# The sums of the token weights leave for DRAM in six pieces, spread over a later stretch of the program, in place of one piece

## The chip, the cores and the metric

The kernel runs on one core of a Trainium2 chip. The core has a matrix engine (TensorE, PE in the profile), a vector engine (VectorE, DVE), an activation engine (ScalarE, ACT), a general engine (GpSimd, POOL) and a synchronisation engine (SyncE, SP) that mostly issues transfers. DMA transfers are issued by SP, ACT and POOL, each on a queue of its own. The metric is the device time of one launch in microseconds (us), lower is better, as the median of several runs. All arithmetic here is float32.

## The reference, cut to what matters

Two blocks stand one behind the other. The first filters a sequence of 3008 positions in the frequency domain, for each of 8 batches and 256 channels; the second is an MLP mixer on the result, first over positions ("tokens"), then over channels.

```python
X = np.fft.rfft(x, axis=1)                       # x: (8, 3008, 256)
y = np.fft.irfft(X * (filt_r + 1j * filt_i), n=3008, axis=1)
xt = y.transpose(0, 2, 1)
h = np.maximum(xt @ w_tok1, 0.0) @ w_tok2        # (3008, 256), (256, 3008)
u = y + h.transpose(0, 2, 1)
h2 = np.maximum(u @ w_ch1, 0.0) @ w_ch2          # (256, 1536), (1536, 256)
return (u + h2).astype(np.float32)
```

The weights arrive as 64-bit floats and are turned into float32 on the chip.

## The kernel before, in words

**The filter.** The transforms are done as matrix products in two stages. The batches form five groups (`GROUPS`, L56: batch 0; 1 and 2; 3 and 4; 5 and 6; 7), and `dft` (L557) runs one group. It is a generator: each `yield` ends a small step. First come the "a" units: rows of `x` are loaded by SP into the three buffers `filts` (L489), multiplied by a table on TensorE (L530), copied by ScalarE and written to a DRAM scratch `z_tmp` (L537 to L541). Then the same three buffers are cleared by GpSimd (L694) and used for the filter's values. For each of 16 pairs `c` SP issues eight loads of filter rows (`filt_pair`, L221 to L228), one load of a table and the loads of `z_tmp` into a tile `t` (`t2_load`, L621 to L632: eight for the first pair, four for each later one). `b_pair` (L668) multiplies the table by `t` on TensorE (L523) and by the filter on VectorE (L674); `join` and `bi_pair` follow, and the result goes to another scratch, `g_tmp` (L689).

**The mixer.** `mix` (L1046) is the main loop. It runs over 288 items, which the code counts with `i`: 8 batches, in each 6 column blocks `m` of up to 512 positions, in each 6 pairs `jp` of channel tiles ("channel pairs"). An item is a fixed series of TensorE products (L936, L970, L952), with the VectorE additions of a fast 2x2 product scheme (L914) and ScalarE's relu (L957) between them. Each item has three places at which the loop at the bottom of the program puts in one step of the next group's `dft`. So the filter for batches 1 and 2 runs between the products of batch 0. The order is written out by hand (`tc.manual_schedule()`), each engine executes its own instructions in that order, and the waits between engines follow from the tiles.

**Token weights.** Batch 0 uses the first token weight directly, as `w1` in SBUF. From batch 1 on the same 2x2 scheme is used, which needs, for each of 12 pairs of slices (`AP`), seven matrices: three that are slices of `w1` as they are and four sums. They are made once while batch 0 runs and kept in a DRAM scratch, `w1_d` (`w1_tmp`). `w1_sums` (L755) returns the list of steps: the raw slices are written to DRAM (L761, L762), sixteen GpSimd operations make the sums in place (L765), and `sums_out` (L773) writes all of them with one DMA from the GpSimd queue (L774). The loop takes one step at item 4 and up to six at each of items 5, 6 and 7 (L1080 to L1083), so that the sums and the DMA are done with item 7. In the program's order that is just behind the last "a" units of group (1, 2), ahead of the clearing of `filts` (L694) on GpSimd. The seven matrices of a pair are read back by `w1_load` (L778) on the SP queue into the same SBUF space, from item 25 on (L1123).

**The second token weight** is treated alike, but already one step per item: `to_dram` (L1074) holds 24 closures of `w2_sums` (L878), four for each `m`: the raw parts to DRAM (L887, L888), two additions (L884), two more (L895, L884), the sums to DRAM (L900). One is taken at the end of each item from item 8 on (L1142).

**Results.** `finish` (L973) adds up a column block and writes it to the output by 16 DMAs on the GpSimd queue (L1017).

Of the kernel before, what the change touches and what calls it, by code (L numbers as in the profile page):

```python
# [42 lines left out]
JP = JT // 2  # L43
# [8 lines left out]
AP = A // 2  # L52
# [75 lines left out]
def kernel(  # L128
# [11 lines left out]
    nc = tc.nc  # L140
# [296 lines left out]
    def convert_middle():  # L437
        advance(middle)
        sum_up()

    def convert_end(copy_now=True):
        ended[0] += 1
        advance(end)
        if copy_now:
            copies()
        fill(5)
# [295 lines left out]
    def t4_load(b, c, lo=PARTS[0], hi=P, queue=nc.sync):  # L742
        if lo == 0:
            t4[b, c] = t4p.tile([P, TC4, D], FP32, tag="t4", name="t4")
        queue.dma_start(t4[b, c][lo:hi], rows_of(g_d, b)[lo:hi, ts(c, TC4), :])
# [9 lines left out]
    def w1_sums():  # L755

        w = w1.rearrange("p (j r) (t n) -> p j r t n", r=2, n=P)
        to = w1_d.rearrange("j p s n -> p j s n")

        def raw_out():  # L760
            nc.gpsimd.dma_start(to[:, :, 0], w[:, :, 0, 0])  # L761
            nc.gpsimd.dma_start(to[:, :, 1:3], w[:, :, 1])  # L762

        def pool(out, in0, in1, op):
            return lambda: nc.gpsimd.tensor_tensor(out=out, in0=in0, in1=in1, op=op)  # L765

        todo = [raw_out]
        for j in range(0, AP, 3):
            c11, c21, c12, c22 = (w[:, j:j + 3, r, t] for r in range(2) for t in range(2))
            todo += [pool(c22, c21, c22, ALU.add), pool(c21, c11, c21, ALU.subtract),  # L770
                     pool(c11, c22, c11, ALU.subtract), pool(c12, c12, c11, ALU.subtract)]

        def sums_out():  # L773
            nc.gpsimd.dma_start(to[:, :, 3:7], w.rearrange("p j r t n -> p j (r t) n"))  # L774

        return todo + [sums_out]

    def w1_load(j):  # L778
        nc.sync.dma_start(w1_ring[:, j % W1S], w1_d[j])
# [94 lines left out]
    def w2m_load(m):  # L874
        hw = width(m) // 2
        nc.sync.dma_start(w2m[m % 2][:, :, 0:hw], w2_d[m, :, :, 0:hw])

    def w2_sums(m):  # L878

        w = width(m)  # L880
        hw = w // 2
        r = w2[:, :, ds(m * 512, w)]
        b11, b12, b21, b22 = (r[:, t, ds(j * hw, hw)] for t in range(2) for j in range(2))
        sub = lambda out, in0, in1: nc.gpsimd.tensor_tensor(out=out, in0=in0, in1=in1, op=ALU.subtract)  # L884

        def raw_out():
            nc.gpsimd.dma_start(w2_d[m, :, 0, 0:hw], b11)  # L887
            nc.gpsimd.dma_start(w2_d[m, :, 1:3, 0:hw], r[:, 1, :].rearrange("p (s n) -> p s n", s=2))  # L888

        def t13():  # L890
            sub(b22, b22, b12)
            sub(b12, b12, b11)

        def t24():
            nc.gpsimd.tensor_tensor(out=b11, in0=b22, in1=b11, op=ALU.add)  # L895
            sub(b21, b11, b21)

        def sums_out():
            for t in range(2):
                nc.gpsimd.dma_start(w2_d[m, :, ds(3 + 2 * t, 2), 0:hw], r[:, t, :].rearrange("p (s n) -> p s n", s=2))  # L900

        return [raw_out, t13, t24, sums_out]
# [122 lines left out]
    def u_part(b, m, i):  # L1025
        if i == 0:
            uts[b, m] = up.tile([P, DH, 512], FP32, tag="u", name="u")
        (u_quarter if b else u_unit)(b, m, h1s[b], uts[b, m], i)

    def v_steps(b, m):  # L1030
        vts[b, m] = vp.tile([P, 4, 256], FP32, tag="v", name="v")
        t13, t2, t4_ = u_sums(uts[b, m], vts[b, m], width(m))

        def t24():
            t2()
            t4_()

        return [t13, t24]
# [7 lines left out]
    def mix(next_ready):  # L1046

        wait = []
        pos, hhs, tts = {}, {}, {}

        def loads(b):
            if b + 1 < B and next_ready(b):
                for c in wait:
                    t4_load(b + 1, c)
                wait.clear()


        own = ({(4, 2): (0, 1)}, {(3, 0): (0,), (4, 0): (1,), (4, 2): (2, 3)})
        new = {(JP - 2, 0): (0, 1), (JP - 1, 0): (2, 3)}

        def u_parts(b, m, jp, place):
            parts = own[b > 0] if m + 1 < MT else new if b + 1 < B else {}
            now = parts.get((jp, place), ())
            b, m = (b, m + 1) if m + 1 < MT else (b + 1, 0)
            for part in now:
                u_part(b, m, part)
            if now and now[-1] == max(p for ps in parts.values() for p in ps):
                if m:
                    wait.append(m)
                todo_v.extend(v_steps(b, m))  # L1070
                if b and (b, m) < (B - 1, MT - 2):
                    w2m_load((m + 2) % MT)

        to_dram = [f for m in range(MT) for f in w2_sums(m)]  # L1074
        w1_todo = w1_sums()
        items = [(b, m, jp) for b in range(B) for m in range(MT) for jp in range(JP)]
        n = MT * JP
        for i in range(len(items) + 1):
            now, old = i < len(items), i >= 1
            if JP - 2 <= i < JP + 2:  # L1080
                for _ in range(6 if i > JP - 2 else 1):
                    if w1_todo:
                        w1_todo.pop(0)()  # L1083
            if i and ended[0] < len(tiles):
                convert_middle()
                convert_end(False)
                convert_middle()
            if now:
                b, m, jp = items[i]
                if i % n == 0:  # L1090
                    wait.append(0)
                w = width(m)
                hhs[i] = hp.tile([P, 4, 256], FP32, tag="hh", name="hh")
                g = [bank("pg").rearrange("p (s n) -> p s n", s=2) for _ in range(2)]
                s = up_first(jp, uts[b, m], vts[b, m], w, g)
                up_middle(hhs[i], w, g, s)
            while todo_h1:
                todo_h1.pop()()
            one_step()
            if old:  # L1100
                bo, mo, jo = items[i - 1]
                tts[i - 1] = tp.tile([P, 4, 256], FP32, tag="t", name="t")
                for f in h_sums(hhs[i - 1], tts[i - 1], width(mo)):
                    f()
                down(mo, jo, 0, hhs[i - 1], tts[i - 1], pos.setdefault((bo, mo), []))
            if now:
                u_parts(b, m, jp, 0)
            copies()
            yield b, i % n, 0
            if ended[0] < len(tiles):  # L1110
                if i == 0:
                    convert_middle()
                convert_end(False)
            if now:
                up_last(jp, uts[b, m], vts[b, m], w, g, s, hhs[i])
                if b + 1 < B and i % n == n - 4:
                    t4_sums(b + 1, 0)
            one_step()
            if now and i % n == n - 1:
                one_step()  # L1120
            if now and b + 1 < B:
                if n - 4 - W1S <= i % n < n - 4:
                    w1_load(i % n - (n - 4 - W1S))  # L1123
                if i % n == n - 4:
                    t4_sums(b + 1, 1)
            copies()
            loads(b)
            yield b, i % n, 1
            if old:
                down(mo, jo, 1, hhs.pop(i - 1), tts.pop(i - 1), pos[bo, mo])  # L1130
                if jo == JP - 1:
                    todo_v.extend(finish(bo, mo, uts[bo, mo], pos[bo, mo]))
                    one_step()
                    one_step()
            if now:
                if b + 1 < B and i % n == n - 4:
                    h1s[b + 1] = token_product(b + 1)
                u_parts(b, m, jp, 2)
                if jp == JP - 1:
                    while todo_v and m + 1 == MT:  # L1140
                        one_step()
                if i >= 8 and to_dram:  # L1142
                    to_dram.pop(0)()
                if i in (28, 29):
                    w2m_load(i - 28)
            loads(b)
            yield b, i % n, 2
        while todo_v:
            one_step()

    with tc.manual_schedule():
# [61 lines left out]
        group, todo, done = -1, iter(()), True  # L1213

        def next_ready(b):
            return done or b != GROUPS[group][-1]
# [4 lines left out]
        n = MT * JP  # L1221
        for b, i, place in mix(next_ready):
            if group + 1 < len(GROUPS) and b == GROUPS[group + 1][0]:
# [4 lines left out]
                todo = iter(()) if done else dft(GROUPS[group + 1]) if group else second  # L1228
# [46 lines left out]
```

## Time and profile before

| What | Value |
|---|---|
| Median of 3 runs | 2457.22 us (2456.94 to 2457.75) |
| The profiled execution's own time | 2455.61 us |
| Its span, first to last instruction | 2453.8 us |
| Mean granted TensorE clock | 0.993 |
| TensorE busy | 2402.2 us, 98% of the span |
| VectorE busy | 1937.0 us, 79% |
| ScalarE, GpSimd busy | 687.3 us, 28%; 620.9 us, 25% |
| The write of the sums (L774) | 3072 KB, issued at 217.1 us, 1084 ns on GpSimd, 13.3 us to landing |

Times inside the profile count from the start of the span. The profile shows, for each engine, what ended its idle time; for TensorE nearly all of the span is work, so that any place where it stood still is of interest. "Granted clock" is the share of the full clock at which TensorE ran. A matmul's end is modelled, since matmuls are pipelined.

### The profile page before, as it was taken

Reading aid. Unit: us, or ns where it says so; the run is one execution under the profiler, and the core shown is the slowest. Engines: PE = TensorE matmul, PEld = TensorE weight load, DVE = VectorE, ACT = ScalarE, POOL = GpSimd, SP = SyncE. Lnnn points to the kernel's source line nnn. Section 1 sums busy time; section 2 is a strip of 40 time slices with the busy share of each in tenths; the row PEclk is TensorE's granted clock in tenths of the full one; section 3 lists DMA queues with packets and bytes.
Section 4 is the critical chain, followed back from the end, with each engine's and each line's share of the span. In section 5 each row is a group of like instructions: output and inputs, shape, how many; then the busy total and the mean of one; then the engine's idle time right before and its main releaser. Section 6 shows DMA issues by size and latency. Waiting matters only on the chain.

```text
span 2453.8 us, 35566 instructions
## 1 busy us (share of the span) xinstructions
PE 2402.2 (98%) x12340; PEld 1973.3 (80%) x12340; DVE 1937.0 (79%) x3684; ACT 687.3 (28%) x1355; POOL 620.9 (25%) x1110
## 2 busy tenths in 40 slices
PE   7998999999999999999999999999999999999998
PEld 4665676977878787987888878897888888898887
DVE  7796878787887888778888888777788788777776
ACT  5742222133222222123221222213222222212222
POOL 7486233113111211211121112112212112112121
PEclk8999999999999999999999999999999999999999
DMA  9986446453443322535344223433325121411100
GB/s 215 247 232 201 123 126 179 147 161 116 121 138 90 86 82 73 167 109 168 94 121 129 86 69 84 155 93 118 98 82 150 50 71 46 148 63 30 39 15 20
DMA packets 187339, 278.65 MB, mean 114 GB/s; under 512 B 35405, under 2 KB 125211, under 8 KB 187160
## 3 DMA queue, kind: packets, MB, share of 16 engines
q1 hardware_dynamic: 140952, 212.56, 29.2%
q0 software_dynamic: 34608, 53.83, 8.2%
q10 hardware_dynamic: 11600, 10.00, 1.3%
q8 instruction: 98, 1.61, 0.3%
q14 instruction: 81, 0.66, 0.1%
HBM read 193.52 MB, written 82.72 MB: 113 GB/s over the span
## 4 chain that ended last, share of the span: by engine, by line
PE 87%; DVE 6%; DMA 3%; issue 1%; ACT 1%; POOL 1%; SPq 0%; ACTq 0%; DVEq 0%; POOLq 0%
PE ps_po L970 33%; PE ps_pg L936 18%; PE ps_pg L952 14%; PE ps_b L523 5%; PE ps_b L802 3%; PE ps_acc L857 3%; PE ps_acc L802 2%; PE ps_b L857 2%; PE ps_b L835 2%; PE ps_acc L835 2%; DVE t L914 1%; PE ps_acc L523 1%; DVE hh L914 1%; PE ps_b L751 1%; DVE u L914 1%
## 5 line engine op out<-in xcount | busy, mean ns | idle before, releaser
L1017 POOL DMA_DIRECT2D out_dram<-r x752 | 409.5, 553 | 1647.4 <-ACT hh L957 1135.5
L914 DVE TENSOR_TENSOR hh<-ps_pg,s 128x512 f32<-128x512 f32 (+3 forms) x864 | 481.6, 585 | 233.3 <-ACT s L939 230.7
L957 ACT ACTIVATE hh<-hh 128x512 f32<-128x512 f32 (+1 forms) x576 | 347.7, 621 | 949.6 <-DVE hh L914 949.6
L970 PE MATMUL ps_po<-t,wc 128*128 128x256 f32 (+1 forms) x2304 | 548.1, 381 | 4.7 <-DVE t L914 3.8
L970 PEld LDWEIGHTS ps_po<-t,wc 128*128 128x128 f32 x2304 | 427.5, 190 | 131.5 <-DVE t L914 44.2
L970 PE MATMUL ps_po<-hh,wc 128*128 128x256 f32 (+1 forms) x1728 | 414.0, 375 | 1.4 <-POOL wc L382 0.8
L936 PE MATMUL ps_pg<-v,wc 128*128 128x256 f32 (+1 forms) x1728 | 413.5, 375 | 0.1
L970 PEld LDWEIGHTS ps_po<-hh,wc 128*128 128x128 f32 x1728 | 326.5, 190 | 42.9 <-ACT s L939 3.6
L936 PEld LDWEIGHTS ps_pg<-v,wc 128*128 128x128 f32 x1728 | 326.8, 190 | 40.9 <-DVE v L914 3.0
L952 PE MATMUL ps_pg<-u,wc 128*128 128x256 f32 (+1 forms) x1152 | 295.2, 379 | 0.7 <-DVE hh L914 0.7
L914 DVE TENSOR_TENSOR t<-t,hh 128x256 f32<-128x256 f32 (+1 forms) x576 | 246.6, 428 | 19.8
L952 PEld LDWEIGHTS ps_pg<-u,wc 128*128 128x128 f32 x1152 | 214.9, 190 | 57.6 <-DVE hh L914 25.1
L914 DVE TENSOR_TENSOR s<-ps_pg,hh 128x512 f32<-128x512 f32 (+1 forms) x288 | 196.0, 681 | 30.7 <-DVE hh L914 0.9
L939 ACT COPY s<-ps_pg 128x256 f32<-128x256 f32 (+1 forms) x288 | 106.0, 368 | 346.2 <-PE ps_pg L936 343.3
L914 DVE TENSOR_TENSOR t<-hh 128x512 f32<-128x512 f32 (+1 forms) x288 | 193.4, 672 | 0.6 <-ACT hh L957 0.6
L936 PE MATMUL ps_pg<-u,wc 128*128 128x256 f32 (+1 forms) x576 | 171.8, 380 | 3.9 <-DVE hh L914 3.9
L952 PE MATMUL ps_pg<-v,wc 128*128 128x256 f32 (+1 forms) x576 | 168.8, 375 | 0.0
L936 PEld LDWEIGHTS ps_pg<-u,wc 128*128 128x128 f32 x576 | 106.3, 190 | 35.6 <-DVE hh L914 20.5
L914 DVE TENSOR_TENSOR u<-ps_acc,u 128x256 f32<-128x256 f32 (+1 forms) x84 | 46.2, 550 | 93.9 <-PE ps_acc L857 86.5
L952 PEld LDWEIGHTS ps_pg<-v,wc 128*128 128x128 f32 x576 | 109.2, 190 | 12.5
L914 DVE TENSOR_TENSOR u<-ps_b,u 128x512 f32<-128x512 f32 (+2 forms) x126 | 74.4, 591 | 28.9 <-PE ps_b L857 26.7
L857 PE MATMUL ps_acc<-w 128*128 128x256 f32 (+1 forms) x336 | 85.2, 376 | 0.0
(149 smaller groups left out, 2716.4 us busy)
## 6 DMA issues: line engine op xcount, KB each, us to landing
w<-w_tmp SPq DMA_DIRECT2D x84, 448.0 KB
w<-w_tmp SPq DMA_DIRECT2D x35, 896.0 KB
out_dram<-r POOLq DMA_DIRECT2D x696, 32.0 KB, 3.2
t<-g_tmp SPq DMA_DIRECT2D x42, 512.0 KB
g_tmp<-t SPq DMA_DIRECT2D x96, 192.0 KB
t<-z_tmp SPq DMA_DIRECT2D x180, 96.0 KB
z_tmp<-t SPq DMA_DIRECT2D x60, 256.0 KB
filt<-in_x_dram SPq DMA_DIRECT2D x90, 128.0 KB
```

Source lines behind the costliest of these rows:

```text
L523: nc.tensor.matmul(outs(i, j), stat(i, j), mov(i, j), start=True, stop=True)
L751: nc.tensor.matmul(acc[:, t, :], w1[:, a, ts(t, P)], t4[b, a // TC4][:, a % TC4, :], start=(a == 0 and t == 0), stop=(a == A - 1 and t == ...
L802: nc.tensor.matmul(ps[:, at], w[:, n], mov, start=(j == 0 and i in (0, 2)), stop=(j == AP - 1 and i >= 5))
L835: nc.tensor.matmul(ps[:, ds(q * P, n)], t4[b, c][:, r, ts(dh, P)], wai[:, 0:n], start=(first and q == 0), stop=(not first and q == 3))
L857: nc.tensor.matmul(ps[:, ds(j * hw, hw)], h1[:, n, :], w2m[m % 2][:, at, 0:hw], start=(i < 2 and j == 0), stop=(j == len(todo) - 1))
L914: nc.vector.tensor_tensor(out=out, in0=in0, in1=in1, op=op)
L936: nc.tensor.matmul(ps[:, 0:hw], chan[0][:, jp, n, :], mov, start=True, stop=True)
L939: nc.scalar.copy(out=s[:, 0], in_=g[0][:, 0, 0:hw])
L952: nc.tensor.matmul(ps[:, 0:hw], chan[0][:, jp, n, :], mov, start=True, stop=True)
L957: nc.scalar.activation(out=hs, in_=hs, func=AF.Relu)
L970: nc.tensor.matmul(po[i][:, j, 0:hw], chan[1][:, jp, n, :], mov, start=(jp == 0 and first == 1), stop=(jp == JP - 1 and last == 1))
L1017: q.dma_start(bass.AP(tensor=ob.tensor, offset=ob.offset + row * D + g * cw, ap=[[N1 * D, 32], [D if h else -D, n], [1, cw]]), blocks[ts(g ...
```

## The change

The one DMA of the sums is cut into six, each for two of the twelve pairs. `w1_sums` returns two lists, the raw write with the sixteen operations, and the six DMAs. The loop takes the first list as before (items 4 to 7), and then one DMA at the start of items 13, 15, 17, 19, 21 and 23. The sixteen operations, the place of `w1_load` and all else stay.

```diff
-        def sums_out():
-            nc.gpsimd.dma_start(to[:, :, 3:7], w.rearrange("p j r t n -> p j (r t) n"))
-
-        return todo + [sums_out]
+        def sums_out(j):
+            return lambda: nc.gpsimd.dma_start(to[:, j:j + 2, 3:7], w[:, j:j + 2].rearrange("p j r t n -> p j (r t) n"))
+
+        return todo, [sums_out(j) for j in range(0, AP, 2)]
...
-        w1_todo = w1_sums()
+        w1_todo, w1_out = w1_sums()
...
                 for _ in range(6 if i > JP - 2 else 1):
                     if w1_todo:
                         w1_todo.pop(0)()
+            elif i >= 2 * JP and i % 2 and w1_out:
+                w1_out.pop(0)()
```

In the GpSimd queue the DMA thereby leaves its place between the sixteen operations and the clearing of `filts`. The six pieces stand among the steps of the second token weight: behind the raw writes of its blocks 1, 2 and 3 (one piece each) and ahead of the writes of their sums (one piece each).

## The prediction

> **What bounds the kernel now.** I read the page first, for the engine that fills the span, then that engine's waits, then the chain and the windows around the longest wait that lies near the change.
>
> ```profile
> span 2453.8 us, 35566 instructions
> PE 2402.2 (98%) x12340; PEld 1973.3 (80%) x12340; DVE 1937.0 (79%) x3684; ACT 687.3 (28%) x1355; POOL 620.9 (25%) x1110
> ```
>
> TensorE is the bound: only 51.6 us of the span are not its work. The list of TensorE's waits over the whole span says where they are:
>
> ```profile
> PE ps_pg L636 <- issue: 10.2, 1, 10.2
> PE ps_b L523 <- DMA t<-z_tmp: 7.2, 1, 7.2
> ```
>
> (Total us, times, longest.) The first is in the opening phase, long before the change. The second is the first `b_pair` of group (1, 2), waiting for loads of `z_tmp`. It is the longest stall inside the mixer. The chain that ended last, between 190 and 260 us, leads to it:
>
> ```profile
> 218.76 0.30 SPq L226
> 219.06 0.05 issue
> 219.11 1.25 SPq L228
> ...
> 221.66 8.34 DMA filt<-in_filt_r_dram
> 230.02 0.30 SPq L632
> 230.31 0.05 issue
> 230.36 2.26 DMA t<-z_tmp
> 232.63 0.04 issue
> 232.67 2.35 PE ps_b L523 x4
> ```
>
> The first filter load leaves SP at 218.76, and one load then needs 8.34 us, against 2.26 for the `z_tmp` load later in the chain. What else runs then is in the answer for line 774, and in the DMA queues from 224 to 228 us (packets, MB, share of 16 engines):
>
> ```profile
> L774 POOL DMA_DIRECT2D w_tmp<-w x1: 1084/1084/1084, 217.1 to 217.1; - x1
> DMA to landing us min/median/max: 13.3/13.3/13.3
> ```
> ```profile
> q0 software_dynamic: 354, 1.42, 93.1%
> q1 hardware_dynamic: 107, 0.08, 6.1%
> ```
>
> The 3072 KB of sums are in flight from 217.1 to about 230.4 us, and GpSimd's queue q0 takes 93% of the engines while SP's q1 gets 6%. The loads that TensorE needs next are the ones in q1. The windows give the second half of the price (the fields are busy us of PE, PEld, DVE, ACT, POOL, then the granted clock):
>
> ```profile
> 226.00:228.00 2.00, 0.00 (x0) 0.00 (x0) 1.57 (x3) 1.23 (x2) 0.00 (x0) 1.00 0.98 359
> 230.00:232.00 2.00, 0.00 (x0) 0.00 (x0) 0.00 (x0) 0.00 (x0) 2.00 (x4) 0.50 0.55 139
> 239.00:240.00 1.00, 1.00 (x4) 0.82 (x3) 0.33 (x1) 0.00 (x0) 0.00 (x0) 0.52 0.83 278
> 240.00:241.00 1.00, 1.00 (x7) 0.87 (x6) 0.00 (x0) 0.00 (x0) 0.00 (x0) 1.00 0.69 212
> ```
>
> While TensorE stands still its clock falls to half, and it stays there until just before 240 us. So a stall of 7.2 us is followed by some 7 us of work at half speed.
>
> **What the Trainium skill says.** DMA: Bandwidth & Descriptors, section on queues, rings and completion order: each DMA engine goes round-robin between the queues that have work, a whole packet at a time. The trace agrees in direction: packets of q0 average 4.0 KB in that window and those of q1 0.75 KB, so equal turns already give q0 five times the bytes. TensorE: Matmul & The Clock Gate, section on what is actually happening: the clock is halved after an idle window of about 3.4 us, counted in a free-running window, and restored after about as long a busy one. The trace agrees for the fall (idle from 225.43; the window from 228 to 230 us has a mean clock of 0.93, so that it was halved at about 229.7, after 4.3 us) and shows about 7 us of work at half clock before the restoration.
>
> **The change part by part.**
>
> *Removed from 217.1 us: the write, on the GpSimd engine.* 1.08 us. Behind it on GpSimd is the clearing of `filts` (three of 0.54 us, the first from 218.19 to 218.73), and SP's first filter load waits for that. Without the write it can leave at 218.76 - 1.08 = 217.68.
>
> *Removed: the traffic.* How fast eight filter loads and eight `z_tmp` loads go when nothing is in the way is shown by group (3, 4): SP issues the first filter load at 612.66 and the last `z_tmp` load at 619.41 (0.36 long), 7.11 us in all, in which one issue took 1.39 us for no reason that I see. From issue to TensorE's start I take what the stalled case itself shows at its end: the fourth `z_tmp` load was out of SP at 231.13 and the matmuls that need it started at 232.67 (1.54 us); for the last load 232.76 and 234.38 (1.62 us). Moved to 217.68: the last load issued at 224.8, usable at 226.4; the first half, 2.3 us earlier in SP's order, at about 224. The writes of `z_tmp` must have landed too: the last is issued at 217.94, and with q0 empty its 256 KB need about as long as the one issued at 215.42, whose packets end near 217.2; so about 220 to 221, no later than SP's turn. TensorE is free for the first half at 225.43 (end of the last L952 product). It therefore starts `b_pair` at once and waits at most 0.5 us for the second half; I take 0.4. That is far below the 4.3 us of idleness after which the clock fell here, so the clock stays up.
>
> *The sum on TensorE.* From 225.43 to the next item's first product (L936, 240.11) the trace has 14.68 us. The work in it is one `b_pair` and eight L970 products. One item later the same work takes 245.74 to 248.59 = 2.85 us. Difference: 14.68 - 2.85 = 11.83 us (7.2 idle, about 4.6 half clock). Less 0.4 for the second half above. VectorE is next: it is free at 227.57, needs 2.44 us for the two L674 products and 1.37 for the two of `join`, so to 231.4, then 0.42 and 0.69 us before L952 may overwrite its banks, 232.6. TensorE, starting its item at 228.3, would be there after 1.73 + 1.29 + 1.02 = 4.04 us, at 232.3. So 0.3 to 0.4 us is lost to VectorE; I take 0.4. Net 11.0 us. Nothing later gives it back: from 240 to 430 us TensorE waits 0.9 us, and from 425 to the end 3.4 us.
>
> *Added: six issues on GpSimd.* Nearest rows: writes of 128 to 256 KB (L887, L888, L900) take 0.54 to 0.56 us of it. 6 x 0.55 = 3.3 us, less the 1.08 removed. Hidden: GpSimd waits 96.5 us for work at L1017 between 245 and 420 us. If that cover were gone, output writes would be 0.55 us later each, and the next block needs the tile they read only about 50 us later.
>
> *Added: six transfers of 512 KB.* Between 13.3/6 = 2.2 us and, by the skill's page on DMA (section on the anatomy of one DMA: about 2.0 us, and a further one per 436 KB), an estimate of 3.2 us. By GpSimd's order in the trace they leave near 249, 304, 306, 314, 356 and 364 us, the later five about 11 us earlier after the change. SP's loads near 304 and 356 are for the pair after next: each pair's loads are issued right after the `b_pair` two before it (291 for the one at 318, and 299 for the one at 333), so they have over 15 us to spare. Two pieces and the neighbouring writes of the second weight are about 2 MB, 9 us at the rate above. I take 0; bounds -0.5 (less crowding elsewhere) and +3 us (a late load).
>
> *The wait at the other end.* `w1_load` on SP needs the pieces landed, with SP's filter and `z_tmp` loads queued behind it. It is first issued at 389.6 us and its fifth at 415.3, the last piece lands near 368. 20 us of slack in the same order of events; 0.
>
> *Sum:* 2453.8 - 11.0 = 2442.8 us of span. The profiled execution lies 1.81 us above its span (2455.61) and the median 1.61 above that; the median becomes **2446.2 us**, -0.45%.
>
> **The rivals.**
>
> *The loads are late anyway.* Then SP's own issuing or the writes of `z_tmp` set the pace, and only part is won. For it: in group (3, 4) the sixteen issues take 7.1 us, and here only 7.75 us lie between 217.68 and 225.43. Against it: half of the loads suffices to start. With 3 us of idleness and full clock: gain 11.83 - 3.0 - 0.4 = 8.4, 2448.8 us. Over about 4.3 us the clock falls too: 11.83 - 4.3 - 4.6 = 2.9, 2454.3 us.
>
> *The sums were not the cause.* If the filter loads are slow for themselves (23 to 24 KB in short rows), only the 1.08 us on GpSimd is won: 2456.1 us. Against it: the same loads in group (3, 4) issue at 0.4 us each.
>
> *Slower: a new stall.* The pieces that leave in pairs near 304 us crowd out SP's loads for a later `b_pair`, as the one write does now. Up to 15 us of lateness it costs nothing; beyond that TensorE waits, and over 4.3 us the half clock comes with it. To end on the other side it must give back 11 us and more, a full second stall of 7.2 + 4.6, and some: lateness of over 22 us for pieces worth 4.4 us of traffic, say 2463 us. Against it: the same place carries 1.1 MB of the second weight now, with no wait of TensorE.
>
> **How the numbers follow.** Full gain 0.72 (own range 2444.3 to 2448.3), part of it 0.13 (2448.3 to 2454.5), no cause 0.07 (2455 to 2458), slower 0.08. The measurement tells about 0.2%, 4.9 us: below 2452.3 is faster. Full gain and most of the partial case: 0.83 faster. The rest of the partial case and "no cause": 0.09 same. 0.08 slower. The range from 2444.2 to 2453.0 leaves out about 0.06 below, and 0.08 + 0.07 and a little of the partial case above.
>
> **What the new profile would show.** Right: no wait of TensorE at L523 over 1 us near 226; clock 1.00 throughout 226 to 240; SP's first filter load near 217.7, the following at 0.3 to 0.4 us each; the first L936 behind it near 228.5 to 229; six L774 issues of about 0.55 us; no new wait of TensorE from 230 to 420 us; every later event about 11 us earlier. Wrong: L523 still waiting over 3 us there, with the clock halved; a wait on `t<-z_tmp` or `filt` near 290 to 360; SP held at `w1_load` by `w_tmp<-w`.

## The result and the profile after

The changed kernel takes 2445.61 us (median of 5 runs, 2444.26 to 2447.52) against 2456.94 us before (5 runs, 2456.41 to 2457.75): a ratio of 0.9955 with a 95% interval of 0.9941 to 0.9970. The forecast was 2446.2 us. The same changed kernel in a later round came to 2446.68 against 2456.13 us (experiment `after_again` below). The profiled execution has a span of 2443.8 us, 10.0 us less than before, and its own time lies 1.81 us above the span, as it did before.

The page of the changed kernel, its first lines:

```profile
span 2443.8 us, 35574 instructions
PE 2399.8 (98%) x12340; PEld 1971.9 (81%) x12340; DVE 1937.0 (79%) x3684; ACT 687.0 (28%) x1355; POOL 621.0 (25%) x1115
```

TensorE's busy time fell by only 2.4 us, the span by 10.0. What went is mostly waiting, as the list of TensorE's waits over the whole span of the changed kernel shows (total us, times, longest):

```profile
PE ps_pg L636 <- issue: 10.8, 1, 10.8
...
PE ps_b L523 <- DVE p L679: 0.7, 2, 0.4
```

The wait of 7.2 us at L523 for `t<-z_tmp` is gone; the only one left at that line is 0.7 us in all, for VectorE. The chain that ended last goes straight through TensorE where it went through SP and two transfers before (start, us, what):

```profile
225.32 1.29 PE ps_pg L952 x6
226.61 0.58 PE ps_b L523 x2
...
228.20 1.92 PE ps_po L970 x8
230.12 1.73 PE ps_pg L936 x8
```

`b_pair` starts in the moment in which the L952 products end, 226.61 us. The windows show the clock (field before the last two) at 1.00 throughout:

```profile
226.00:228.00 2.00, 2.00 (x11) 0.73 (x9) 1.93 (x5) 0.43 (x1) 0.00 (x0) 1.00 0.47 123
230.00:232.00 2.00, 2.00 (x11) 1.77 (x10) 1.97 (x3) 0.37 (x1) 2.00 (x4) 1.00 0.65 190
238.00:240.00 2.00, 2.00 (x11) 1.76 (x10) 1.97 (x3) 0.37 (x1) 1.64 (x3) 1.00 0.83 213
```

The six writes, in the answer for line 774:

```profile
L774 POOL DMA_DIRECT2D w_tmp<-w x6: 715/724/732, 249.7 to 355.0; - x6
DMA to landing us min/median/max: 3.2/4.6/7.9
```

**A yardstick for the experiments.** The place just ahead of the change, the end of the last L952 products ahead of the first `b_pair`, is reached at 225.43 us before, 226.61 us after, and anywhere from 223.4 to 228.9 us in the other profiled executions (229.9 in one whose edit puts a stall just ahead of it). Much of this shift is there at 155 us, ahead of every edit: the same L952 products start from 2.1 us earlier to 3.3 us later than in the kernel before. So beside the medians I give the *local interval*: from that end to the start of the next item's first L936 product. It is 14.68 us before (225.43 to 240.11) and 3.35 us after (226.61 to 229.96): 11.33 us less. It is not free of the shift: where TensorE comes later against SP's loads, less of their lateness is left for it to wait out (the filler below is such a case).

### The profile page after: what moved, and what is told of

It reads as the page before. It is cut to its first block, busy times and chain, and to the rows that moved or that the text cites. A ratio compares the mean times of both kernels' runs of the same rounds, so it can differ in the third digit from the quotient of the medians.

```text
span 2443.8 us, 35574 instructions
## 1 busy us (share of the span) xinstructions
PE 2399.8 (98%) x12340; PEld 1971.9 (81%) x12340; DVE 1937.0 (79%) x3684; ACT 687.0 (28%) x1355; POOL 621.0 (25%) x1115
## 4 chain that ended last, share of the span: by engine, by line
PE 88%; DVE 6%; DMA 3%; issue 1%; ACT 1%; POOL 0%; SPq 0%; ACTq 0%; DVEq 0%; POOLq 0%
PE ps_po L970 33%; PE ps_pg L936 18%; PE ps_pg L952 14%; PE ps_b L523 5%; PE ps_b L802 3%; PE ps_acc L857 3%; PE ps_acc L802 2%; PE ps_b L857 2%; PE ps_b L835 2%; PE ps_acc L835 2%; DVE t L914 1%; PE ps_acc L523 1%; PE ps_b L751 1%; DVE hh L914 1%; DMA st<-in_moe_w_tok_dram 1%
## 5 line engine op out<-in xcount | busy, mean ns | idle before, releaser
L970 PE MATMUL ps_po<-t,wc 128*128 128x256 f32 (+1 forms) x2304 | 546.8, 380 | 5.0 <-DVE t L914 4.0
L970 PEld LDWEIGHTS ps_po<-t,wc 128*128 128x128 f32 x2304 | 426.4, 190 | 130.9 <-DVE t L914 45.1
L970 PE MATMUL ps_po<-hh,wc 128*128 128x256 f32 (+1 forms) x1728 | 414.0, 375 | 1.4 <-POOL wc L382 0.8
L936 PE MATMUL ps_pg<-v,wc 128*128 128x256 f32 (+1 forms) x1728 | 413.4, 375 | 0.2 <-DVE v L914 0.2
L970 PEld LDWEIGHTS ps_po<-hh,wc 128*128 128x128 f32 x1728 | 326.5, 190 | 42.9 <-ACT s L939 3.4
L936 PEld LDWEIGHTS ps_pg<-v,wc 128*128 128x128 f32 x1728 | 326.8, 190 | 40.9 <-DVE v L914 3.2
L952 PE MATMUL ps_pg<-u,wc 128*128 128x256 f32 (+1 forms) x1152 | 295.2, 379 | 0.6 <-DVE hh L914 0.4
L952 PEld LDWEIGHTS ps_pg<-u,wc 128*128 128x128 f32 x1152 | 214.9, 190 | 57.5 <-DVE hh L914 25.8
L936 PE MATMUL ps_pg<-u,wc 128*128 128x256 f32 (+1 forms) x576 | 171.8, 380 | 3.4 <-DVE hh L914 3.4
L952 PE MATMUL ps_pg<-v,wc 128*128 128x256 f32 (+1 forms) x576 | 168.8, 375 | 0.0
L936 PEld LDWEIGHTS ps_pg<-u,wc 128*128 128x128 f32 x576 | 106.2, 190 | 35.1 <-DVE hh L914 20.1
L952 PEld LDWEIGHTS ps_pg<-v,wc 128*128 128x128 f32 x576 | 109.2, 190 | 12.6
```

The lines of the kernel that those rows point to most:

```text
L936: nc.tensor.matmul(ps[:, 0:hw], chan[0][:, jp, n, :], mov, start=True, stop=True)
L952: nc.tensor.matmul(ps[:, 0:hw], chan[0][:, jp, n, :], mov, start=True, stop=True)
L970: nc.tensor.matmul(po[i][:, j, 0:hw], chan[1][:, jp, n, :], mov, start=(jp == 0 and first == 1), stop=(jp == JP - 1 and last == 1))
```

## The experiments

The theory: the 3072 KB of sums crowd out the small loads that the first `b_pair` of group (1, 2) needs; TensorE waits, and its clock falls. Rivals: the cut into pieces matters, and not the place; the place in GpSimd's queue matters, ahead of the clearing of `filts`; or the pieces cost something where they are now.

**Moved, not cut.** One piece at item 13 (`sums_out` takes the number of pairs as a second argument):

```diff
-        return todo, [sums_out(j) for j in range(0, AP, 2)]
+        return todo, [sums_out(0, AP)]
```

> The sums leave in one piece of 3072 KB at item 13, so the write is moved but not cut. If the gain comes from taking the traffic out of the way of the first b_pair of group (1, 2), as I hold, this is worth as much as the change: 2446 us (2444 to 2448), no wait of TensorE at L523 near 226 us. If the cutting is what matters (small pieces let other loads through), the one piece makes a new stall near 250 to 265 us and the time is 2450 us or more.

Measured: 2445.03 us (2443.64 to 2448.23), ratio 0.9959 (0.9946 to 0.9971); local interval 3.47 us. From 228 to 420 us its TensorE waits show one line:

```profile
PE ps_b L523 <- DVE p L679: 1.1, 3, 0.4
```

The one write, issued at 252.3 us and 12.3 us to landing, does no harm there. The whole gain comes from the move; the cut adds nothing that these runs can tell.

**Cut, not moved.** Six pieces at item 7:

```diff
-        return todo, [sums_out(j) for j in range(0, AP, 2)]
+        return todo + [sums_out(j) for j in range(0, AP, 2)], []
...
-                for _ in range(6 if i > JP - 2 else 1):
+                for _ in range((1, 6, 6, 10)[i - JP + 2]):
```

> The six pieces of 512 KB leave at item 7, one behind the other, where the one write stood: cut but not moved. My theory: the same 3072 KB are in flight at the same time, and the clearing of filts on GpSimd stands behind six issues of 0.7 us in place of one of 1.1 us, so about 3.2 us later. The stall stays and grows by up to 3 us: 2457 to 2460 us. If the cutting is what matters: 2446 to 2452 us.

Measured: 2456.87 us (2455.68 to 2457.78), ratio 1.0001 (0.9993 to 1.0009); local interval 15.02 us. TensorE's wait:

```profile
PE ps_b L523 <- DMA t<-z_tmp: 7.9, 1, 7.9
```

The stall stays, so cutting is not the cause. I had forecast 2457 to 2460 us; the wait grew by 0.6 us only (7.87 against 7.23), and the median not measurably. GpSimd spent 4.41 us on the six issues, so that SP's first filter load left about 3 us later against TensorE, and yet `b_pair` started only 0.6 us later: the first load does not set the start by itself. Neither does the end of the traffic: `b_pair` starts 2.3 us behind the landing of the write in the kernel before and 3.9 us behind that of the last piece here.

**The one write behind the clearing.** GpSimd clears `filts` first and issues the whole write then:

```diff
                 nc.gpsimd.memset(filts[c][:, :, 0, :], 0.0)
+        while behind_clear:
+            behind_clear.pop()()
...
+        behind_clear.append(sums_out(0, AP))
+        return todo, []
```

> The one write stands right behind the clearing of filts on GpSimd, some 2 us later than before: SP's first filter load is freed by the GpSimd issue (1.1 us earlier), the traffic stays beside the loads. If the traffic is the cause: the stall stays at 5 to 8 us with the half clock behind it, 2455 to 2459 us. If the place in GpSimd's queue ahead of the clearing is the cause: 2446 to 2448 us.

Measured: 2455.07 us (2452.85 to 2457.26), ratio 0.9995 (0.9987 to 1.0003); local interval 13.00 us. SP's queue in this run (start, us):

```profile
219.57 0.31 SPq L226 DMA_DIRECT2D filt<-in_filt_r_dram  x1
...
224.22 1.88 SPq L632 DMA_DIRECT2D t<-z_tmp  x1
226.16 1.20 SPq L631 DMA_DIRECT2D t<-z_tmp  x1
```

Now all eight filter loads are issued at their usual 0.2 to 0.4 us each, as the write is issued at 220.5 and its packets flow from about 222.3, and it is the first six of the eight `z_tmp` loads that take 0.8 to 1.9 us each to issue. TensorE still waits 6.0 us and its clock falls. The place ahead of the clearing is not the cause; the write in flight beside the loads is. Whether the same bytes would do so from SP's or ScalarE's queue was not tried.

**Half of the traffic.** 1536 KB at item 7, the rest at item 13:

```diff
-        return todo, [sums_out(j) for j in range(0, AP, 2)]
+        return todo + [sums_out(0, AP // 2)], [sums_out(AP // 2, AP // 2)]
```

> Half of the sums (1536 KB) leave at item 7 as before, half at item 13. If the traffic is the cause, its end comes about 6 us earlier than with the whole, near 224 us, and the first b_pair starts near 227.5 to 229 us in place of 232.7. Idleness of 2 to 3.5 us is below the 4.3 us after which the clock fell, so no half clock: 2449 us (2447.5 to 2451). If the clock falls all the same: 2453 to 2454 us. If any big write there costs the whole stall: 2457 us.

Measured: 2453.61 us (2449.30 to 2457.52), ratio 0.9990 (0.9983 to 0.9996); local interval 11.79 us. My 2449 us was wrong; the line I had named for a falling clock is what came. The wait and the windows:

```profile
PE ps_b L523 <- DMA t<-z_tmp: 4.4, 1, 4.4
```
```profile
226.00:228.00 2.00, 0.12 (x1) 0.00 (x0) 1.98 (x4) 0.92 (x2) 0.00 (x0) 1.00 0.03 6
230.00:232.00 2.00, 1.52 (x4) 0.37 (x4) 0.00 (x0) 0.00 (x0) 2.00 (x5) 0.71 0.62 162
236.00:238.00 2.00, 2.00 (x7) 1.62 (x6) 1.23 (x2) 0.00 (x0) 1.61 (x3) 0.58 0.73 216
```

Two things are to be seen. The wait shrank only from 7.2 to 4.4 us, although half of the traffic was gone and over by about 223.5 us: SP waits 2.5 us for a filter load, until 226.88 us, while the DMA engines are 29% busy from 224 to 226 us and 3% from 226 to 228. And the clock falls at about 230.8 us (0.71 over that window), when TensorE is already at work again.

**The clock alone.** The kernel before, with eight products that need no load ahead of that `b_pair`:

```diff
             pss, wb, t2 = two_banks(), wbs[c], t2s[c]
+            if bs == GROUPS[1] and c == 0:
+                for _ in range(8):
+                    nc.tensor.matmul(pss[0].rearrange("p b d -> p (b d)"), wai,
+                                     chan[0][:, 0, 0:4, :].rearrange("p n i -> p (n i)"), start=True, stop=True)
```

> The kernel before, with eight more products of 128x512 (0.86 us each, 6.9 us in all) on TensorE right ahead of the first b_pair of group (1, 2); their result is overwritten. They fill the stall and need no load. My theory holds that 4.6 of the 11.8 us are the half clock behind the stall: with the filler the clock stays up, b_pair starts at about 232.7 us as before, and the time is 4 to 4.6 us under before (about 2452 us). If the clock costs nothing of its own: no change, or slower by what the filler exceeds the stall.

Measured: 2453.69 us (2451.89 to 2458.27) against 2456.13, ratio 0.9989 (0.9981 to 0.9997), so 2.4 us (0.7 to 4.7), short of the 4 to 4.6 forecast; local interval 10.63 us, 4.05 us less than before. TensorE and the clock in this run (each product has two records):

```profile
227.18 7.03 PE L672 MATMUL ps_b<-wc,wai 128*128 128x512 f32 x16
234.14 1.07 PE L523 MATMUL ps_b<-t,wb 48*64 48x512 f32 x3
234.62 0.61 PE L523 MATMUL ps_acc<-t,wb 48*64 48x512 f32 x1
```
```profile
234.00:236.00 2.00, 2.00 (x9) 0.57 (x8) 0.65 (x1) 0.00 (x0) 2.00 (x4) 1.00 0.63 179
```

TensorE is busy through the whole stall, and the clock stays at 1.00. The 4.05 us are not the clock's alone, though, as TensorE reached the place later against SP's loads here. The second half of `b_pair` (the `ps_acc` products) waits for the later `z_tmp` loads in both runs: the trace has the seventh of the eight loads landed at 234.24 before and at 234.49 with the filler, 0.14 and 0.13 us ahead of it. In the kernel before it starts at 234.38:

```profile
234.38 2.37 PE L523 MATMUL ps_acc<-t,wb 48*64 48x512 f32 x4
```

That is 8.95 us behind the end of the L952 products (225.43); with the filler it is 7.28 us (234.62 - 227.34). So 1.67 us are an earlier arrival of the loads. From there to the next L936 product it takes 5.73 us at half clock (240.11 - 234.38) and 3.35 us at full clock (237.97 - 234.62): that is 2.4 us for the clock, an estimate from one execution of each, and the medians say 2.4 us too. That the filler ran until 234.2, past the first loads that `b_pair` needs, adds little, since the later loads set the end.

So the 11.83 us that the forecast found in this place are 7.2 us of idleness, by this estimate 2.2 us in which `b_pair` waits for its later loads, and 2.4 us of half clock: a fifth of the price, where the forecast had 4.6 us.

**Twice the pieces.** The changed kernel, each piece written a second time to a scratch that nobody reads:

```diff
+                for d in (w1_d, w1_copy):
+                    nc.gpsimd.dma_start(d.rearrange("j p s n -> p j s n")[:, j:j + 2, 3:7], ...)
```

> The changed kernel with each of the six pieces written a second time, to a scratch that nobody reads: 3072 KB more of traffic and six more issues on GpSimd, in the same places. If the pieces are hidden where they stand now: as the changed kernel, 2444 to 2447 us. If they cost something there, that cost doubles: 2448 us or more, with a wait of TensorE between 240 and 380 us.

Measured: 2445.35 us (2444.07 to 2446.74), ratio 0.9953 (0.9940 to 0.9965); local interval 3.40 us. TensorE's waits from 225 to 420 us are 1.3 us in all, against 0.7 in the changed kernel and 1.2 in its repetition. Another 3072 KB at these places cost nothing measurable, so neither do the first.

**The changed kernel again**, on the chip of the last two.

> The changed kernel itself, for a comparison on the same chip: 2444 to 2447 us. Its profiled execution above was 1.2 us late already before the place of the change (217 us); if that is chance, the events before 217 us come on average no later than in the kernel before.

Measured: 2446.68 us (2443.71 to 2449.51), ratio 0.9959 (0.9947 to 0.9972); local interval 3.34 us. In this execution TensorE reached the place of the change at 228.91 us, 3.5 us later than in the kernel before, and with doubled pieces at 223.42: a shift from ahead of the change that the runs show in both directions, large enough to account for the spread of the changed kernel's times (3.3 us in its first five runs, 5.8 in these). What makes it vary was not looked into. The expectation that these events come no later on average stays open: both executions of the changed kernel are later (1.2 and 3.5 us), the one with doubled pieces is 2.0 us earlier.

**Why the loads stay late after the traffic.** In the run with half of the sums early, a reading offered itself: a filter load of 23 rows might lie on a single DMA engine. The first trial cut it in two:

```diff
-                nc.sync.dma_start(t[to + 32:to + 32 + n, i, 0], raw(src, row, [[64 * D, n], [1, D]]))
+                for j, m in ((0, 16), (16, n - 16)) if cut and n == A - 1 else ((0, n),):
+                    nc.sync.dma_start(t[to + 32 + j:to + 32 + j + m, i, 0], raw(src, row + 64 * j, [[64 * D, m], [1, D]]))
```

> As with half of the sums at item 7 and half at item 13, but the filter loads of 23 rows of the first pair are cut into 16 and 7 rows (two loads more). With half of the sums early the DMA engines stood almost idle from 225 to 228 us while SP waited 2.5 us for a filter load, whose packets followed each other 42 ns apart and more, one at a time: I read this as a load of 23 rows that lies on one DMA engine. If so, the wait of 2.5 us goes, two issues are added, b_pair starts 1.5 to 2 us earlier; where the idle time of TensorE is then too short for the clock to fall the time is 2447 to 2450 us, else about 2452. If the load was late for another reason: 2453 to 2454 us as without the cut.

Measured: 2451.46 us (2449.68 to 2454.73), ratio 0.9981 (0.9973 to 0.9988), and no answer. The two added loads changed which earlier transfer other transfers wait for, and a new wait arose on ScalarE, in front of the relu:

```profile
ACT hh L958 <- DMA filt<-in_filt_r_dram: 8.3, 1, 8.3
```

ScalarE's last write of `z_tmp` was held until a filter load had landed, and TensorE stood 4.6 us at L971 for the relu behind it. So the trial was made again without a change in the number of loads, 16 rows in place of 23 (seven rows of each of the two loads are left out):

```diff
-                n, row = (A - 1, 64 - k) if k else (A, 32)
+                n, row = (16 if few else A - 1, 64 - k) if k else (A, 32)
```

> As with half of the sums at item 7 and half at item 13, but the two filter loads of 23 rows of the first pair load 16 rows (7 rows each are left out, so a few frequencies of batches 1 and 2 are missing); number and order of all loads and waits stay. If a load of 23 rows lies on one DMA engine and that is what SP waited 2.5 us for while the engines stood almost idle, the wait goes, b_pair starts 2 to 2.5 us earlier than with 23 rows, and the idle time of TensorE falls from 4.4 us to 2 to 2.5: 2447 to 2449.5 us where the clock then stays up, 2451 us where it does not. If the load was late for another reason: 2453 to 2454 us as with 23 rows.

Measured: 2452.07 us (2450.52 to 2455.41), ratio 0.9983 (0.9976 to 0.9990) against 0.9990 (0.9983 to 0.9996) with 23 rows; TensorE's wait is 3.7 us. SP's wait is still there:

```profile
SPq L228 <- DMA filt<-in_filt_r_dram: 2.3, 1, 2.3
```

2.3 us in place of 2.5: the reading falls for that wait. In the last microsecond before SP goes on (223.5 to 224.5) SP's queue holds this share of the engines:

```profile
q1 hardware_dynamic: 16, 0.01, 6.1%
```

6.1% is close to 1 in 16: on average one DMA engine is at work, though each of the cut loads has only 16 rows. This fits one engine that lags behind the others after the burst; the view doesn't name engines, and why is not settled.

The same cut in the kernel before, with all of the sums in one piece at item 7:

> The kernel before with the same two loads cut to 16 rows (7 rows each left out). In the kernel before the chain goes through a load of 23 rows (8.34 us). If that load's single engine adds to the stall beside the traffic, the first b_pair starts about 1.7 us earlier and the time is 1 to 3 us less, with the half clock still there: 2453.5 to 2455.5 us. If the traffic alone sets the start, no difference: 2456 to 2457 us. If the single engine were the whole cause: 2446 us.

Measured: 2455.91 us (2454.61 to 2458.48), ratio 0.9999 (0.9991 to 1.0007); local interval 14.08 us, TensorE's wait 6.3 us. The expected 1 to 3 us do not show: 0.6 us in one local interval, nothing in the ratio, whose interval still allows up to 2.2 us. The long 23-row load in the chain of the kernel before was in the main a victim of the traffic; as a second cause it is not seen, and a small share is not excluded.

| Kernel | Median, us | Ratio | TensorE waits at L523 for `z_tmp` | Local interval |
|---|---|---|---|---|
| before | 2456.94 | 1 | 7.2 | 14.68 |
| changed | 2445.61 | 0.9955 | 0 | 3.35 |
| moved, not cut | 2445.03 | 0.9959 | 0 | 3.47 |
| cut, not moved | 2456.87 | 1.0001 | 7.9 | 15.02 |
| behind the clearing | 2455.07 | 0.9995 | 6.0 | 13.00 |
| half early | 2453.61 | 0.9990 | 4.4 | 11.79 |
| filler on TensorE | 2453.69 | 0.9989 | 0 (filled) | 10.63 |
| pieces twice | 2445.35 | 0.9953 | 0 | 3.40 |

## Why the prediction was right

**The bound and the stall.** Right. The one stall inside the mixer was the traffic's doing; moving it away is the whole gain, and 11.33 us of local interval went where 11.0 were forecast (medians: 2445.61 against 2446.2; that they lie within 0.6 us is in part luck, as the five runs of the changed kernel span 3.3 us).

**The first filter load.** Forecast for 217.68, seen at 217.52, with the next ones 0.2 to 0.4 us each. The match says less than it seems, since TensorE came 1.18 us later in this execution: against the end of its L952 products the load was 9.09 us ahead, where 7.75 were forecast.

**The writes of `z_tmp`.** This step was wrong: they were to land "no later than SP's turn". SP's waits in the changed kernel have

```profile
SPq L631 <- DMA z_tmp<-t: 1.4, 1, 1.4
```

The last write was issued at 219.13 and SP's first `z_tmp` load left at 222.47, 3.3 us later, where I had allowed 2 to 3. With the traffic gone, this is now what sets SP's pace. It used up most of what SP had gained on TensorE, but cost little: `b_pair` took 1.59 us to the L970 products, 1.02 one item later, so 0.57 us in place of the 0.4 taken for the late second half.

**VectorE.** Wrong by its 0.4 us: from L936 (229.96) to L952 (234.09) the changed kernel needs 4.13 us, and 4.14 in the next item (238.43 to 242.57). Nothing was lost. This error and the 0.17 us of the last paragraph cancel in part: 11.83 - 0.57 = 11.26, against 11.33 measured.

**The half clock.** Mis-sized: 4.6 of the 11.83 us were put down to it, and the filler and the traces give about 2.4. The rest, some 2.2 us, was waiting inside `b_pair` for the later loads. The sum did not suffer, as 11.83 is the difference of two intervals, whatever its parts are. For the same reason the right sum is no test of this term. The 1.54 us from issue to use has a related flaw: by the chain that the prediction shows, the start at 232.67 followed the third `z_tmp` load, issued at 230.36, and not the fourth. As a threshold ("over about 4.3 us the clock falls too") the half clock failed as well: with half early and 16 rows the wait was 3.7 us, and the clock fell 2.4 us into it. With half of the sums early it was the wait that I had wrong, 4.4 us where I counted on 2 to 3.5.

**The pieces.** Sized too low, hidden all the same: 0.72 us of GpSimd each, not 0.55, and 3.2 to 7.9 us to landing where 2.2 to 3.2 were estimated. The doubled pieces show that this is hidden. `w1_load` waited 0.2 us in all for a write to `w_tmp` (the profile leaves out the number, so the scratch of the second weight has this name too), as good as the 0 of the sum. Its load at 415.3 us in the kernel before is the fourth and not the fifth, which changes nothing.

**The rivals.** "The sums were not the cause" falls with the run that moves them and does nothing else. "The loads are late anyway" came in small: the writes of `z_tmp` do set SP's pace in the changed kernel, at 0.57 us of the second half in place of 3. In the run with half of the traffic, lateness remained after the traffic. "A new stall" did not come, even with twice the pieces.

## What to carry to other kernels

A large write that nobody waits for is not free: look at what is loaded while it is in flight, and who needs that first. Move it to a stretch in which loads are issued well ahead of their use, before thinking of its size: here one piece of 3072 KB did as well there as six. Half of its bytes, left where they were, kept most of the stall (4.4 of 7.2 us). And price a stall of TensorE with what follows it: here 7.2 us of waiting cost 11.3 us, about 2.4 of them half clock.

## What the runs showed of the hardware

**When the clock falls and comes back.** From the mean clocks of the windows, the clock in the kernel before fell at 229.72 us (0.93 from 228 to 230) and came back at 239.96 (0.52 from 239 to 240). For all runs with a stall, in us, by the clock records of the traces:

| Kernel | Last product ahead of the stall ends | Clock falls | Clock is back | At half |
|---|---|---|---|---|
| before | 225.43 | 229.72 | 239.96 | 10.24 |
| cut, not moved | 224.17 | 226.76 | 240.41 | 13.65 |
| behind the clearing | 227.69 | 232.00 | 242.24 | 10.24 |
| half early | 226.12 | 230.84 | 237.66 | 6.82 |
| half early, loads cut | 220.81 | 226.11 | 229.52 | 3.41 |
| half early, 16 rows | 224.03 | 226.41 | 236.65 | 10.24 |
| before, 16 rows | 224.14 | 229.22 | 239.46 | 10.24 |

The time at half clock is one, two, three or four times 3.41 us, so the clock changes in steps of about that length. This fits the free-running window of about 3.4 us of which the Trainium skill tells (TensorE: Matmul & The Clock Gate, section on what is actually happening). The time from the last product to the fall varies with the place of the stall in these steps, from 2.4 to 5.3 us. A step need not be wholly idle for the clock to fall: where the fall came after 2.6 and 2.4 us, TensorE had still worked for the first 0.8 and 1.0 us of the 3.41 us ahead of it.

The return took 7.2 to 9.0 us of work from the first product of `b_pair`, but 3.1 to 5.1 us from the first L970 product behind it, the first one on the full 128 rows. In the run with the cut loads, where the stall stood ahead of L971 products on the full 128 rows, it was 4.1 us from the first of these. In the kernel before, the 3.41 us from 233.13 to 236.54 are filled with `b_pair` products alone and left the clock at half; the next 3.41, filled with L970 products, brought it back. That products on 48 rows hardly count as activity would explain this; it was not tried by itself.

**Issuing gets slower under a burst.** SP mostly needs 0.2 to 0.4 us to issue one of these loads, and for most of them 0.8 to 1.9 us while a burst from GpSimd's queue fills the engines, whichever load it is (the filter loads before, the `z_tmp` loads where the write stood behind the clearing). In the kernel before, the eight filter loads took 8.84 us to issue (218.76 to 227.60) and 3.22 us in the changed one (217.52 to 220.74), so this is a large part of the delay. Not every issue under the burst is slow: those at 226.33 and 228.00 took 0.30 us each. What holds an issue up was not looked into.

**A burst has a tail.** After half of the sums had left, SP waited 2.3 to 2.5 us more for loads, on engines that fell almost idle meanwhile (3% busy from 226 to 228 us with half early), on average with one engine in sixteen at work at the end of the run with 16 rows. Its cause is open.
